# Placing the Gram products of a ConvNeXt-V2 block by the kind of slot, in portions of five

## The chip, the cores and the metric

The kernel runs on one core of one Trainium2 chip. The metric is the device time of one execution in microseconds. The engines are called TensorE (PE in the profile, its weight loads PEld), VectorE (DVE), ScalarE (ACT), GpSimd (POOL) and SyncE (SP, which issues DMAs). They run at the same time, each through its own instructions in program order, and wait for each other by semaphores.

## What is computed

One image of 512 x 512 pixels with C = 96 channels goes through a depthwise 3x3 convolution, a layer norm over channels, a matrix product to E = 384 channels, GELU, a global response normalization (GRN, which needs the sum of squares of each of the 384 channels over all pixels), and a product back to 96 channels, with the input added:

```python
out = sum over i, j of xp[:, i:i+H, j:j+W, :] * dw[i, j]      # depthwise 3x3
h = _layernorm(out)                                           # eps 1e-5
h = gelu(einsum('bhwc,ce->bhwe', h, w1))
gx = sqrt((h * h).sum(axis=(1, 2)) + 1e-6)
nx = gx / (gx.mean(axis=-1) + 1e-6)
h = grn_gamma * (h * nx) + grn_beta + h
return x + einsum('bhwe,ec->bhwc', h, w2)
```

## The kernel before

The image is cut into 128 blocks of four rows. Because GRN needs a sum over the whole image before the second product, the kernel has two parts. The first (to about 950 us of the span) does convolution, norm, first product, GELU and the sums of squares; the second makes the output, and makes most of the GELU output again. The change touches the first part.

The first part is a loop over slots s. In a slot the convolution works on block s, the first product and GELU on a block about 14 slots older, and the norm's steps on blocks between. The instructions of each engine stand in the order in which the code writes them (class `InOrder`), so the place of a call in the slot is its place in the engine's queue.

**PSUM.** The tile `PS` has eight banks of 512 f32 columns. Banks 0 to 3 take the first product's units, banks 4 to 6 the convolution's sums (`Y3`), bank 7 (`SG`, L398 to L400) two things: the norm's statistics `S` and the Gram sums `gram`.

**Units** (`unit`, L755). A block's first product is 12 banks, written as units 0 to 5 of one bank, unit 6 and unit 8 of two banks, and units 10 and 11 of one. After each, ScalarE makes one GELU pass over the one or two banks. Unit n lies in bank n mod 4, so it waits for the pass that emptied that bank.

**Taps** (`conv_taps`, L500 on; `conv` in the slot). The convolution is 72 small matmuls in three bursts of 24, called `conv(0)` ahead of unit 0, `conv(1)` behind unit 3 and `conv(2)` behind unit 6. In most slots `conv(1, u0)` waits for the GELU pass of unit 0 and `conv(2, u4)` for that of unit 4.

**Evacuation** (`evac`, L521). Behind the third burst the three banks of sums are copied to SBUF. There are two kinds of slot, told apart at L971: in a *shared* slot ScalarE copies two banks and VectorE the third; in the other kind, called a *three-bank slot* here, ScalarE copies all three in one pass. Which one a slot is depends on the block whose first product it makes: `cm_quads(b) == 2` makes it shared. From slot 20 on, counted by the last digit of that block's number, slots 0, 2, 3, 6 and 7 are three-bank slots and 1, 4, 5, 8 and 9 are shared. There are 54 three-bank slots from there to the end of the convolution; 33 follow a shared slot and 21 another three-bank slot.

**Sums of squares.** A block's GELU output comes in four quarters. For `cm_quads(b)` of them, channels lie on partitions and VectorE takes the sums (`squares`, `bn_stats`). For the rest pixels lie on partitions, and TensorE forms Gram products: a 128 x 128 matmul of a piece of the output with itself, added into `gram`, whose diagonal is wanted at the end. Each such quarter makes 12 Gram products, so a block makes 24, 12 or none. `owe_grams` (L815) puts them in a list when the block is done, and `gram_next(n)` (L808) writes the next n of the list into TensorE's queue, fewer if there are fewer. A block's output tile is one of five in a ring (`gpool`).

**Statistics.** In each slot 24 matmuls with `rowsel` add the norm's sums into `S` (`stage_stats`). Once in four slots VectorE copies `S` out and sets it to zero (`stage_moments`, the zeroing at L560). The first Gram product written after a zeroing waits for it, as both are in bank 7.

**The early slots.** Slots 5, 6, 8 and 9 make first products, slots 7 and 10 to 17 do not (the hole: the norm of the next blocks is not ready). A slot without units writes `gram_next(12)` first of all (L929), ahead of its taps. From slot 128 on there is no convolution, and up to 12 Gram products follow each unit (`mlp_tail`, L707).

Of the kernel before, what the change touches and what calls it, by code (L numbers as in the profile page):

```python
# [19 lines left out]
WHOLE = (0, 3, 7)  # L20
NTAIL = 14
GRB = 3
PORTION = 4


class InOrder:
# [31 lines left out]
def kernel(  # L58
# [40 lines left out]
    def is_whole(q):  # L99
        return q < TAIL0 and q % 10 in WHOLE or q == TAIL0  # L100
# [102 lines left out]
    with ExitStack() as p1:  # L203
# [428 lines left out]
        def stage_turn(k):  # L632
            NT = (BATCHES[k][1] * GR * NG + 31) // 32 * 32
            rt = rtpool.tile([128, NS], bf16, name="rt")
            dve.transpose(out=rt[:, :NT], in_=rns.pop(k)[:, :NT])
            rts[k] = rt
# [59 lines left out]
        def quarter(b, t):  # L696
            return gs[b][t] if isinstance(gs[b], list) else gs[b][:, t]
# [110 lines left out]
        def gram_next(n):  # L808
            for b, c0, j in grams[:n]:
                c = c0 % QC + j * 128  # L810
                v = quarter(b, c0 // QC).rearrange("p j w -> p (j w)")[:, c:c + 128]
                pe.matmul(gram[:, j, :], lhsT=v, rhs=v, start=False, stop=True, skip_group_check=True)
            del grams[:n]
# [37 lines left out]
        for k, (b0, n) in enumerate(BATCHES):  # L851
# [16 lines left out]
            for b in range(b0, b0 + n):  # L868
# [7 lines left out]
                put(m + is_whole(b), "combine", b)  # L876
                last_slot = m

        loaded = [4]
        busy(FILL[1])  # L880
        turn_x(0)
# [2 lines left out]
        for s in range(last_slot + 1):  # L884
            get = lambda kind: at.get((s, kind), [])
            early = s < AHEAD
            while loaded[0] < min(s + (6 if early else 5), NBLK):
                load_x(loaded[0])
                loaded[0] += 1
            if early:  # L890
                for b in get("read"):
                    stage_read(b)
            for k in get("rows"):
                stage_rows(k)
            for k in get("bcast"):
                stage_bcast(k)
            if not early:
                for b in get("read"):
                    stage_read(b)
            for b in get("write"):  # L900
                stage_write(b)
            if not HOLE <= s < HOLE + 4:
                store_next()
            if any(b >= TAIL0 for b in get("mlp")):
                store_next()
            for k in get("newton"):
                stage_newton(k, pool)
            for b in get("sqp"):
                stage_sq(b, False)
            for b in get("norm"):  # L910
                stage_norm(b)
            for k in get("rstd"):
                stage_rstd(k, pool)
            mlp = get("mlp")

            def spread_out(bank=0):
                for k in get("spread"):
                    stage_spread(k, bank)
                for b in get("norma"):
                    stage_norm(b, dve if b < 2 else pool)  # L920

            spare = not mlp and s % 2 == 1
            taps, evac = conv_taps(s, spare) if s < NBLK else ([], None)
            if mlp and mlp[0] >= TAIL0:
                assert not taps
                square_owed()
                mlp_tail(mlp[0], get)
            elif not mlp:
                gram_next(12)  # L929
                if s + 3 < NBLK and s != RAMP:  # L930
                    turn_x(s + 3)
                halves = [(b, h) for b in get("stats") if b >= RAMP for h in range(2)]
                for n, f in enumerate(taps):
                    f()
                    if n < 2:
                        for b, h in halves[:2 if len(halves) > 2 else 1]:
                            stage_stats(b, (h,))
                        del halves[:2 if len(halves) > 2 else 1]
                if not spare:
                    spread_out()  # L940
                if s == 3:
                    setup_mlp()
                if evac:
                    evac(s == RAMP)
                if s == RAMP:
                    turn_x(s + 3)
                for b in get("sqa"):
                    stage_sq(b, True)
                for b in get("stats"):
                    if b < RAMP:  # L950
                        stage_stats(b)
                for k in get("moments"):
                    stage_moments(k)
                if spare:
                    spread_out()
                for k in get("chain"):
                    stage_moments(k)
                    stage_chain(k)
                for k in get("turn"):
                    stage_turn(k)  # L960
                square_owed()
            else:
                b = mlp[0]
                unit, squares, squares_rest = mlp_units(b)
                lone = s - 1 not in mlp_slots

                def conv(n, behind=None):
                    if taps:
                        taps[n](lone, None if lone else behind)

                shared = evac is not None and (cm_quads(b) == 2 or s < HOLE)  # L971

                def turn():
                    if s + 3 < NBLK:
                        turn_x(s + 3)

                conv(0)
                u0 = unit(0, 1)
                unit(1, 1)
                if shared:  # L980
                    turn()
                    gram_next(PORTION)
                unit(2, 1)
                squares(0)
                gram_next(PORTION)
                unit(3, 1)
                conv(1, u0)
                spread_out(2)
                u4 = unit(4, 1)
                squares(1)  # L990
                gram_next(PORTION)
                unit(5, 1)
                if not shared:
                    turn()
                unit(6, 2)
                if not shared:
                    squares(2)
                    gram_next(PORTION)
                if s >= LATE:
                    for k in get("turn"):  # L1000
                        stage_turn(k)
                conv(2, u4)
                if evac:
                    evac(shared)
                if shared:
                    squares(2)
                else:
                    gram_next(PORTION)
                unit(8, 2)
                if shared:  # L1010
                    for b2 in get("stats"):
                        stage_stats(b2)
                unit(10, 1)
                if shared:
                    gram_next(PORTION)
                unit(11, 1)
                if not shared:
                    for b2 in get("stats"):
                        stage_stats(b2)
                for k in get("moments"):  # L1020
                    stage_moments(k)
                squares_rest(2)
                square_owed()
                if s < LATE:
                    for k in get("turn"):
                        stage_turn(k)
                if is_whole(b):
                    owed.append(lambda f=squares_rest: f(3))
                owe_grams(b, cm_quads(b) * QC, NQ * QC)
                if is_whole(b):  # L1030
                    stores.extend((b, h) for h in range(3))
            if s == 0:
                setup_ynt()
            if s == 4:
                setup_rest()
            if s == 6:
                for i in range(NI):
                    sp.dma_start(out=w1s[i:128:4], in_=w1p[i:C:NI])
            for b in get("combine"):
                combine(b)  # L1040
            if s == last_slot - 3:
                pc.close()
                late.gr = p2.enter_context(tc.tile_pool(name="gr", side="right", bufs=GRB))
                late.gh = p2.enter_context(tc.tile_pool(name="gh", side="right", bufs=1))
                late.xr = p2.enter_context(tc.tile_pool(name="xr", side="right", bufs=5))
                late.o = p2.enter_context(tc.tile_pool(name="o", side="right", bufs=6))
            if s == last_slot - 2:
                for n in range(XPRE):
                    load_xr(n, sp)
            if s == last_slot:  # L1050
                for n in range(PRE):
                    load_g(n, sp)
                for n in range(YPRE):
                    load_yn(n, sp)
# [109 lines left out]
```

## Time and profile before

| | us |
|---|---|
| median of 3 runs | 1436.2 (1435.39 to 1436.63) |
| the profiled execution | 1436.17 |
| its span in the profile | 1434.2 |
| TensorE busy | 1383.6 (96%) |
| ScalarE busy | 1380.3 (96%) |
| VectorE busy | 1306.3 (91%) |
| GpSimd busy | 887.8 (62%) |
| Gram products, 1632 of them, busy | 159.0 |
| three-bank evacuations from 100 to 865 us | 54, of 1.45 each |

Busy time is that in which an engine had at least one instruction under way. Matmuls overlap: one of 128 columns shows 0.22 us, but in a row the next one starts 0.056 us after it. For what work costs an engine, starts of neighbours are compared, not durations. The span is what the profile shows of an execution; the execution's own time is 2.0 us longer.

### The profile page before, as it was taken

Reading aid. Unit: us, or ns where it says so; the run is one execution under the profiler, and the core shown is the slowest. Engines: PE = TensorE matmul, PEld = TensorE weight load, DVE = VectorE, ACT = ScalarE, POOL = GpSimd, SP = SyncE. Lnnn points to the kernel's source line nnn. Section 1 sums busy time; section 2 is a strip of 40 time slices with the busy share of each in tenths; the row PEclk is TensorE's granted clock in tenths of the full one; section 3 lists DMA queues with packets and bytes.
Section 4 is the critical chain, followed back from the end, with each engine's and each line's share of the span. In section 5 each row is a group of like instructions: output and inputs, shape, how many; then the busy total and the mean of one; then the engine's idle time right before and its main releaser. Section 6 shows DMA issues by size and latency. Waiting matters only on the chain.

```text
span 1434.2 us, 54995 instructions
## 1 busy us (share of the span) xinstructions
PE 1383.6 (96%) x23332; PEld 829.0 (58%) x23332; DVE 1306.3 (91%) x2400; ACT 1380.3 (96%) x1693; POOL 887.8 (62%) x735
## 2 busy tenths in 40 slices
PE   8999999999999999999999997789999999999998
PEld 3445545555555555455545554467777777777776
DVE  8859999999999999999999998988888888888888
ACT  6889989999999999999999999999999999999997
POOL 2559999999998999999999997301111111111110
PEclk9999999999999999999999999999999999999999
DMA  6577899898888899999898987649999999999997
GB/s 194 169 219 222 248 285 274 259 276 271 258 261 251 268 266 272 290 262 268 258 278 270 266 249 221 187 166 411 415 384 412 404 414 398 414 390 392 397 397 279
DMA packets 167565, 423.65 MB, mean 295 GB/s; under 512 B 34166, under 2 KB 83766, under 8 KB 162710
## 3 DMA queue, kind: packets, MB, share of 16 engines
q1 hardware_dynamic: 151652, 314.59, 69.2%
q0 software_dynamic: 15104, 105.39, 18.5%
q8 instruction: 182, 2.98, 0.9%
q14 instruction: 65, 0.53, 0.1%
q10 hardware_dynamic: 562, 0.15, 0.0%
HBM read 262.16 MB, written 157.79 MB: 293 GB/s over the span
## 4 chain that ended last, share of the span: by engine, by line
PE 57%; ACT 19%; DVE 15%; DMA 4%; POOL 2%; issue 2%; SPq 1%; ACTq 0%; POOLq 0%; DVEq 0%
PE PS L36 57%; ACT g L36 14%; DVE bst L36 10%; ACT y_bf L36 4%; DVE xT L36 2%; DMA yn_dram<-yn 2%; DMA g_dram<-g 1%; POOL ysq L36 1%; POOL yn L36 1%; SPq L36 1%; DVE y_bf L36 1%; DVE o_sb L36 1%; DMA xin<-in_x_dram 0%; DVE mom L36 0%; ACT ysq L36 0%
## 5 line engine op out<-in xcount | busy, mean ns | idle before, releaser
L36 ACT ACTIVATE g<-PS 128x512 bf16<-128x512 f32 (+2 forms) x1160 | 704.1, 780 | 8.4 <-PE PS L36 8.1
L36 DVE BATCH_NORM_STATS2 bst<-g 128x6 f32<-128x512 bf16 x1020 | 622.5, 673 | 20.7 <-ACT g L36 20.4
L36 ACT ACTIVATE gr<-PS 128x1536 bf16<-128x1536 f32 x344 | 479.6, 1456 | 14.0 <-PE PS L36 7.8
L36 POOL TENSOR_TENSOR yn<-y_bf,rbc 128x1536 bf16<-128x1536 bf16 x126 | 391.4, 3108 | 61.6 <-ACT rbc L36 23.8
L36 PE MATMUL PS<-ynT,w1p 128*128 128x512 bf16 x1110 | 344.4, 383 | 19.4 <-ACT g L36 9.3
L36 PE MATMUL PS<-xT,Wq 64*32 64x511 bf16 (+1 forms) x9198 | 337.9, 387 | 7.4 <-ACT y_bf L36 0.8
L36 DVE TENSOR_TENSOR o_sb<-PS,B2c 128x384 bf16<-128x384 f32 x512 | 280.0, 555 | 58.4 <-PE PS L36 52.9
L36 POOL TENSOR_TENSOR ysq<-y_bf 128x1536 bf16<-128x1536 bf16 x114 | 313.3, 2748 | 26.0 <-ACT y_bf L36 20.0
L36 PEld LDWEIGHTS <-g 128*128 128x128 bf16 (+1 forms) x3603 | 218.3, 98 | 121.5 <-issue 39.6
L36 PE MATMUL PS<-ynT,w1s 128*128 128x512 bf16 x972 | 262.7, 379 | 0.0
L295 POOL DMA_DIRECT2D xr<-in_x_dram x116 | 62.2, 537 | 286.2 <-DVE o_sb L36 286.2
L36 PEld LDWEIGHTS <-gr 128*128 128x128 bf16 x4104 | 201.0, 98 | 53.8 <-issue 0.7
L36 PE MATMUL PS<-W2s,gr 128*128 128x96 bf16 x4032 | 209.8, 206 | 1.0 <-DVE o_sb L36 0.4
L36 ACT ACTIVATE y_bf<-PS 128x1536 bf16<-128x1536 f32 (+2 forms) x147 | 182.5, 1263 | 13.8 <-PE PS L36 13.2
L36 DVE STREAM_TRANSPOSE xT<-xin 128x576 f32<-128x576 f32 (+1 forms) x256 | 181.6, 749 | 11.0 <-PE PS L36 7.0
L36 PEld LDWEIGHTS <-w1p 128*128 128x128 bf16 x1110 | 95.5, 98 | 162.1 <-issue 114.3
L36 PEld LDWEIGHTS <-Wq 64*32 64x32 bf16 x9216 | 104.9, 90 | 127.4 <-ACT g L36 56.8
L36 PE MATMUL PS<-g 128*128 128x128 bf16 x1632 | 159.0, 220 | 6.4 <-DVE PS L36 5.8
L36 DVE TENSOR_TENSOR o_sb<-o_sb,xr 128x768 bf16<-128x768 bf16 x256 | 142.7, 557 | 8.9
L36 PE MATMUL PS<-w1p,ynT 128*128 128x384 bf16 (+1 forms) x924 | 141.6, 273 | 7.0 <-ACT y_bf L36 2.0
L36 PEld LDWEIGHTS <-ynT 128*128 128x128 bf16 x924 | 73.0, 97 | 59.1 <-issue 36.7
L36 PE MATMUL PS<-W2s,g 128*128 128x96 bf16 x1968 | 103.8, 206 | 0.2
(114 smaller groups left out, 660.3 us busy)
## 6 DMA issues: line engine op xcount, KB each, us to landing
g<-g_dram POOLq DMA_DIRECT2D x36, 1536.0 KB, 9.6
xin<-in_x_dram SPq DMA_DIRECT2D x126, 432.0 KB
g_dram<-g SPq DMA_DIRECT2D x105, 512.0 KB
yn_dram<-yn SPq DMA_DIRECT2D x512, 96.0 KB
ynT<-yn_dram SPq DMA_DIRECT2D x128, 384.0 KB
out_dram<-o_sb SPq DMA_DIRECT2D x127, 384.0 KB
xr<-in_x_dram POOLq DMA_DIRECT2D x124, 384.0 KB, 7.4
ynT<-yn_dram SPq DMA_DIRECT2D x243, 128.0 KB
```

The source lines that it names most:

```text
L36: r = f(*a, **k)
L295: pq.dma_start(out=xr[:], in_=x[0, r0:r0 + GR].rearrange("r w c -> (r w) c").rearrange("(p g) c -> p g c", g=PXP))
```

## The change

`PORTION`, the number of Gram products in a portion, goes from 4 to 5, and the portions move. A flag `was_shared` remembers whether the last slot with units was shared.

| place in the slot | before, shared | before, three-bank | after, shared | after, three-bank |
|---|---|---|---|---|
| behind unit 1 | 4 | | | |
| ahead of unit 3 | 4 | 4 | 5 behind a three-bank slot | 5 behind a three-bank slot |
| behind unit 4 | 4 | 4 | 5 | 5 |
| behind unit 6 | | 4 | | |
| behind the evacuation, ahead of unit 8 | | 4 | | 10 |
| behind unit 8 | | | | 5 |
| behind unit 10 | 4 | | | |

The list of owed products is never lost: what a slot does not write stays for the next. Over ten slots 144 products come in; before there is room for 160, after for 150. The list holds up to 32 between slots before, up to 56 after.

```diff
-PORTION = 4
+PORTION = 5
...
+        was_shared = False
...
                 unit(1, 1)
                 if shared:
                     turn()
-                    gram_next(PORTION)
                 unit(2, 1)
                 squares(0)
-                gram_next(PORTION)
+                if not was_shared:
+                    gram_next(PORTION)
                 unit(3, 1)
                 conv(1, u0)
...
                 unit(6, 2)
                 if not shared:
                     squares(2)
-                    gram_next(PORTION)
...
                 conv(2, u4)
                 if evac:
                     evac(shared)
                 if shared:
                     squares(2)
                 else:
+                    gram_next(2 * PORTION)
+                unit(8, 2)
+                if not shared:
                     gram_next(PORTION)
-                unit(8, 2)
                 if shared:
                     for b2 in get("stats"):
                         stage_stats(b2)
                 unit(10, 1)
-                if shared:
-                    gram_next(PORTION)
                 unit(11, 1)
...
+                was_shared = shared
```

No matmul is added or taken away, and the order of work on the other engines is the same.

## The prediction

> **What bounds the kernel now.** I read the stages first (busy time by stretch), then the groups of the steady stretch with shapes kept apart, then the order of time on TensorE and ScalarE over single slots, then the chain of waits in the early hole. The stretches:
>
> ```profile
> 150.00:400.00 250.00, 244.58 (x4462) 126.05 (x4446) 242.56 (x431) 245.52 (x391) 237.92 (x163) 0.99 0.90 267
> 400.00:650.00 250.00, 246.86 (x4525) 128.32 (x4517) 244.28 (x431) 248.46 (x395) 235.39 (x163) 1.00 0.91 268
> ```
>
> Columns: stretch, TensorE, its weight loads, VectorE, ScalarE, GpSimd busy, then clock and DMA. ScalarE is busy 98 to 99%, VectorE 97 to 98%. So a reordering on TensorE can gain at most what ScalarE idles, and loses as soon as TensorE falls behind ScalarE. The change moves Gram products alone: in the two builds' instruction order only TensorE's differs.
>
> The groups from 150 to 900 us (busy and mean ns, then idle time before and its releaser):
>
> ```profile
> L36 ACT ACTIVATE g<-PS 128x512 bf16<-128x512 f32 x818 | 420.3, 685 | 6.1 <-PE PS L36 5.7
> L36 PE MATMUL PS<-g 128*128 128x128 bf16 x1488 | 145.2, 220 | 6.1 <-DVE PS L36 5.8
> ```
>
> ScalarE's small idle time stands before one-bank passes, and TensorE's waits stand before Gram products, released by "DVE PS": the zeroing of the statistics (L560), which lie in the Gram products' PSUM bank. One such wait, on TensorE and then on VectorE:
>
> ```profile
> 320.80 0.82 PE L36 MATMUL PS<-ynT,w1p 128*128 128x512 bf16 x3
> 322.48 0.38 PE L36 MATMUL PS<-g 128*128 128x128 bf16 x4 [0.86 <-DVE PS L36]
> ...
> 322.27 0.17 DVE L36 MEMSET PS<- 128x128 f32 x1
> ```
>
> The first portion of this three-bank slot (behind a shared one) holds up the fourth unit and the second tap burst.
>
> Now a three-bank slot on TensorE, from its second tap burst to the next slot's:
>
> ```profile
> 510.19 0.88 PE L36 MATMUL PS<-xT,Wq 64*32 64x512 bf16 x24
> 511.01 0.39 PE L36 MATMUL PS<-ynT,w1p 128*128 128x512 bf16 x1
> 511.24 0.39 PE L36 MATMUL PS<-g 128*128 128x128 bf16 x4
> 511.46 0.81 PE L36 MATMUL PS<-ynT,w1p 128*128 128x512 bf16 x3
> 512.11 0.39 PE L36 MATMUL PS<-g 128*128 128x128 bf16 x4
> 512.42 0.87 PE L36 MATMUL PS<-xT,Wq 64*32 64x512 bf16 x24
> 513.23 0.40 PE L36 MATMUL PS<-g 128*128 128x128 bf16 x4
> 513.46 1.03 PE L36 MATMUL PS<-ynT,w1p 128*128 128x512 bf16 x4
> 514.33 0.45 PE L36 MATMUL PS<-rowsel,y_bf 128*128 128x4 bf16 x12
> ...
> 515.00 0.88 PE L36 MATMUL PS<-xT,Wq 64*32 64x512 bf16 x24
> 515.84 0.59 PE L36 MATMUL PS<-ynT,w1p 128*128 128x512 bf16 x2
> ```
>
> Starts are what counts, since ends overlap. Four Gram products take 0.22 us (0.056 each), a bank of units 0.216, a burst of taps 0.80 to 0.85, the 24 statistics 0.67, a switch from full tiles to taps 0.09. The second burst may not start before ScalarE has finished the slot's first unit (L987); here TensorE stood 0.13 us for that.
>
> **The change, part by part.** ScalarE's ends lie 0.49 us apart for one bank and 0.917 for two, in slot after slot; by that slope three banks are 1.344. Without a wait a three-bank slot is then 8 x 0.49 + 2 x 0.917 + 1.344 = 7.10 us and a shared one 8 x 0.49 + 3 x 0.917 = 6.67. From 103 to 865 us ScalarE's ends are 11.3 us later than that: 3.3 at the 54 three-bank evacuations, 0.8 at one late copy of VectorE (558 us), the rest at the zeroings, some 7.2 (the worst one, at 181.8 us, is 4.3).
>
> 1. *The evacuation.* In three-bank slots 8 products lay between the fifth unit and the third burst, now 5: the burst starts 3 x 0.056 = 0.17 us earlier. The evacuation started 0.13 to 0.16 us after the pass before allowed, so all 3.3 us come back. The burst's other condition (the fifth unit's pass) ends some 0.3 us before it in the trace and does not take over. Gain 3.3.
>
> 2. *The zeroing.* Behind a shared slot the portion ahead of the fourth unit is gone; the first product then stands behind the fifth unit, 0.75 (first pass) + 0.05 + 0.82 (burst) + 0.23 (unit) = 1.85 us after the slot's first pass starts. The zeroings end 0.3 to 1.2 us after that start, so six of the seven stalls go; the seventh ended at 2.96 and keeps about 1.1 us. Of 7.2 us 1.1 stay. Gain 6.1. In the other place (a shared slot behind a three-bank one) the zeroing ended about 0.7 us or more before the slot's first pass in all but one case, and nothing changes.
>
> 3. *The loop of a three-bank slot.* From its second burst to the next slot's it now carries 25 products: 5 behind the fifth unit, 10 behind the evacuation, 5 behind the two-bank unit, 5 ahead of the next fourth unit. From the rows: burst 0.82, unit 0.23, five products 0.28, three banks 0.65, switch 0.09, burst 0.81, ten products 0.57, four banks 0.86 with five products 0.28 inside, statistics 0.67, burst 0.84, three banks 0.65, five products 0.28, bank and switch 0.31: 7.34 us of unbroken TensorE work against ScalarE's 7.10. So TensorE becomes the bound here. Behind a shared slot (33 cases) TensorE had been waiting and starts level: the next slot's first unit is written at 5.27 + 0.84 = 6.11, its matmul ends 0.38 later, and a pass begins 0.04 after and takes 0.60: end at 7.13, due at 7.05, so 0.08 lost. The next second burst starts at 7.34 where 7.18 was allowed; the fifth unit ends 0.82 + 0.39 + 0.04 + 0.60 = 1.85 later, at 9.19, due at 7.13 + 4 x 0.49 = 9.09: 0.10 more. A three-bank slot behind another (21 cases) loses the whole 7.34 - 7.10 = 0.24. Cost 33 x 0.18 + 21 x 0.24 = 11.0. As a test of the sum, the trace's own unbroken stretch from that burst to the next slot's first unit, with 12 products in it, takes 5.64 to 5.68 us in four slots; the rows above give 5.27 + 0.84 - 8 x 0.056 = 5.66. With each loop 0.05 shorter the cost would be 33 x 0.08 + 21 x 0.19 = 6.6 (both halves of the 0.18 shrink), with 0.05 longer 33 x 0.28 + 21 x 0.29 = 15.3.
>
> 4. *The shared slots* shed their products (16 or fewer to 5). ScalarE was ahead of nothing there (no excess beyond 0.1 us in its ends); TensorE's loop falls to about 6.4 us against 6.67. It waits longer; gain 0.
>
> 5. *The hole* (slots 10 to 17, no units). Slots 8 and 9 now hand 14 products on; 12 of them open slot 10 and 2 slot 11. The chain of waits runs there through TensorE nearly without a break, from the zeroing on:
>
> ```profile
> 66.07 0.18 DVE PS L36
> 66.25 0.04 issue
> 66.29 1.24 PE PS L36 x29
> ```
>
> Before, slot 10's first burst (from 64.98) ran ahead of this zeroing and only the statistics waited. Now the products wait for it, and the burst is queued behind them on TensorE, and the statistics behind the burst: 12 x 0.056 + 0.09 + 1.0 (burst to statistics) = 1.75 us. The two of slot 11 add two switches, about 0.25. The zeroing itself comes from an unbroken row of VectorE work and is not moved. Cost 2.0. Cover: none, GpSimd was level with TensorE at the hole's end (an evacuation at 93.47 waited for it by 0.1) and so hides at most that much; the first pass behind the hole follows ScalarE's evacuation and square directly.
>
> The grant of the clock is a bound on this. In the trace it was halved for one window of 3.41 us after the 3.0 us wait at 181.8 and after a wait of 1.75 us at 864.7, not after waits of 1.2 us. The new wait at 65 to 66.3 is about 1.3 us, nearest the last: I take 0, with 1.7 (half a window) as the other end. [...]
>
> 6. *The end of the convolution* (slots 128, 129): 20 more products arrive. ScalarE idled 0.94, 0.47 and 0.21 us there while TensorE ran at half clock, so six more products at 0.107 us cost up to 0.7; but the fuller slot 127 shortens the 1.75 us wait that had halved the clock, which can give as much back. I take 0, from -0.7 to +0.7.
>
> Sum: -3.3 - 6.1 + 11.0 + 2.0 = +3.6. The profiled execution took 1436.17 us (span 1434.2), as good as the median of 1436.2: 1439.8.
>
> **The rivals.**
>
> *The loop has room after all* (the products fit behind the evacuation and TensorE is never late): 1436.2 - 3.3 - 6.1 + 2.0 = 1428.8, faster. For it: TensorE's 7.34 us is made of start distances, some of which may hide short waits. Against: the rows would have to shrink by 0.08 us and more, and the stretch that tests them varies by 0.04. It decides from a loop of 7.26 us down: there the cost is 33 x 0.02 + 21 x 0.16 = 4.0 and the sum -3.4. Chance 0.09.
>
> *Loss and gain cancel*: the loop is 0.05 shorter, cost 6.6 instead of 11.0 (1435.4), or the hole costs 1 us instead of 2 because GpSimd or a transfer sets its end after all (1438.8). For it: the sum is a small difference of larger terms. Chance 0.27.
>
> *The zeroing stays a wait.* With the stalls gone VectorE (idle 2 to 3%) loses the time in which it caught up; if it runs 1 us later, the products behind the fifth unit wait for it: six times about 0.5 us and the 0.7 us of a late copy twice, +4.5, 1444. For: its lag at this point already differs from 0.3 to 3.0. Against: three-bank slots become longer than they were, which gives VectorE its time back. Chance 0.08.
>
> *The clock halves in the hole*: 1439.8 + 1.7 = 1441.5. Chance 0.1.
>
> **How the numbers follow.** My forecast, the TensorE loop decides and the kernel gets slower as summed, has 0.46; with the last two rivals slower gets 0.62 (0.02 of the zeroing rival falls within the bound). Within 0.2% (2.9 us, about what a measurement of this kernel can tell from no change) 0.29, faster 0.09. The time is the likeliest case's, 1439.8; its own range, from the loop's 0.03 us either way and the ends of points 5 and 6, is 1439 to 1443.5 (what falls lower is the cancelling case). To leave out no more than 2 in 10, the range goes down to 1435.0, which takes in the cancelling case, and up to 1444.0.
>
> **What would show it.** Right: no TensorE wait of about 1 us on "DVE PS" ahead of Gram products in three-bank slots; three-bank evacuations that start on time; in runs of two three-bank slots a distance of 7.3 to 7.35 us between second bursts, with no wait of TensorE in between, and ScalarE's idle time before the fifth unit's pass; a first pass behind the hole near 98.4 instead of 96.4. Wrong: slots of 7.10 us there, or new waits on VectorE behind the fifth unit, or a hole of the old length.

## The result and the profile after

| | before | after |
|---|---|---|
| median of 20 runs each | 1434.94 us (1429.92 to 1438.37) | 1439.02 us (1435.54 to 1444.06) |
| profiled execution (its span) | 1436.17 us (1434.2) | 1439.77 us (1438.0) |

The ratio of the two, estimated from all the executions of both, is 1.0035, with a 95% interval of 1.0025 to 1.0044: the changed kernel is slower by 5.0 us (3.6 to 6.3). The two medians alone lie 4.1 us apart. The prediction was +3.6 us and 1439.8.

The stretches of the changed kernel's profile (stretch, then busy TensorE, weight loads, VectorE, ScalarE, GpSimd, then clock and DMA):

```profile
150.00:400.00 250.00, 246.36 (x4529) 125.02 (x4527) 245.00 (x435) 249.80 (x397) 236.53 (x163) 1.00 0.91 269
400.00:650.00 250.00, 246.49 (x4531) 125.16 (x4528) 245.31 (x433) 249.77 (x396) 235.71 (x163) 1.00 0.88 266
```

ScalarE now shows as busy without a gap (249.8 of 250), and yet the kernel is slower. The groups of the changed kernel from 150 to 900 us say the same:

```profile
L36 ACT ACTIVATE g<-PS 128x512 bf16<-128x512 f32 x826 | 431.6, 658 | 0.6
L36 PE MATMUL PS<-g 128*128 128x128 bf16 x1513 | 126.1, 219 | 0.0
```

The 6.1 us of idle time that stood before the one-bank passes and the 6.1 us before the Gram products, both of which the prediction started from, are gone. The one-bank passes are busy for 431.6 us instead of 420.3; some 4 us of that are 8 more passes inside the same window. The rest is lateness that doesn't show as idle time. In the records a pass starts ahead of the end of the one before: at the fifth unit of a three-bank slot behind another three-bank slot by 0.18 us before the change (mean of 21 slots), and its end comes 0.49 us after the end before. In the changed kernel that pass starts 0.01 us behind that end and its own end comes 0.60 us after it. A pass that is 0.1 us late thus loses overlap and adds to the busy time. What counts is when the passes end.

I therefore cut the time by ScalarE's records: the *hole stretch* runs from the start of slot 9's first GELU pass to the start of slot 18's, the *steady stretch* from there to the end of slot 127's last pass, the last slot with taps. In us, before and after: hole stretch 36.58 and 42.79, steady stretch 768.21 and 765.50, the rest behind it 569.6 and 568.6, with another 1.3 us ahead of slot 5. So the change gained 2.7 us in the steady stretch of these two executions and lost 6.2 in the hole. The experiments show that the two numbers vary, and that they depend on each other.

### The profile page after: what moved, and what is told of

It is laid out like the page before. It is cut to its first block, busy times and chain, and to the rows that moved or that the text cites. A ratio compares the mean times of both kernels' runs of the same rounds, so it can differ in the third digit from the quotient of the medians.

```text
span 1438.0 us, 54995 instructions
## 1 busy us (share of the span) xinstructions
PE 1383.1 (96%) x23332; PEld 819.6 (57%) x23332; DVE 1307.3 (91%) x2400; ACT 1383.3 (96%) x1693; POOL 887.7 (62%) x735
## 4 chain that ended last, share of the span: by engine, by line
PE 48%; ACT 27%; DVE 16%; DMA 4%; issue 3%; SPq 2%; POOL 1%; ACTq 0%; POOLq 0%
PE PS L36 48%; ACT g L36 20%; DVE bst L36 11%; ACT y_bf L36 6%; DVE xT L36 3%; DMA yn_dram<-yn 2%; SPq L36 2%; DMA rbc<-r_dram 1%; DVE y_bf L36 1%; POOL yn L36 1%; DVE o_sb L36 1%; ACT xT L36 1%; DMA xin<-in_x_dram 0%; ACT ysq L36 0%; DVE mom L36 0%
## 5 line engine op out<-in xcount | busy, mean ns | idle before, releaser
L36 ACT ACTIVATE g<-PS 128x512 bf16<-128x512 f32 (+2 forms) x1160 | 711.5, 757 | 3.8 <-PE PS L36 3.2
L36 PE MATMUL PS<-ynT,w1p 128*128 128x512 bf16 x1110 | 339.1, 382 | 24.9 <-ACT g L36 9.4
L36 PEld LDWEIGHTS <-g 128*128 128x128 bf16 (+1 forms) x3603 | 205.5, 98 | 89.7 <-issue 26.6
L36 DVE STREAM_TRANSPOSE xT<-xin 128x576 f32<-128x576 f32 (+1 forms) x256 | 181.8, 750 | 14.2 <-PE PS L36 14.0
L36 PE MATMUL PS<-g 128*128 128x128 bf16 x1632 | 135.9, 219 | 1.6 <-DVE PS L36 1.2
```

The costliest lines, as they stand in the source:

```text
L36: r = f(*a, **k)
```

## The experiments

"Late" below is the sum, over the steady stretch, of how much later than its ideal pace (7.10 us for a three-bank slot, 6.67 for a shared one) ScalarE ended its passes. Ratios are to the kernel before, run on the same chip beside each; the hole and steady columns come from each one's single profile.

| run | median, us | ratio (95% interval) | hole | steady | late |
|---|---|---|---|---|---|
| before | | | 36.58 | 768.21 | 11.3 |
| after | 1439.02 | 1.0035 (1.0025 to 1.0044) | 42.79 | 765.50 | 8.5 |
| after_again | 1437.57 | 1.0041 (1.0029 to 1.0053) | 40.26 | 764.90 | 7.9 |
| e1_early_as_before | 1433.48 | 1.0003 (0.9991 to 1.0015) | 37.75 | 767.71 | 10.8 |
| e2_ahead_moved | 1433.27 | 0.9995 (0.9982 to 1.0008) | 42.81 | 759.21 | 2.3 |
| e3_evac_only | 1431.47 | 0.9989 (0.9976 to 1.0002) | 40.33 | 761.21 | 4.3 |
| e4_evac_and_zero | 1428.55 | 0.9964 (0.9949 to 0.9978) | 36.57 | 760.37 | 3.4 |
| e5_both | 1426.48 | 0.9970 (0.9959 to 0.9982) | 36.68 | 761.25 | 4.3 |
| e6_hole_only | 1435.37 | 1.0033 (1.0017 to 1.0049) | 40.74 | 763.06 | 6.1 |
| e6_hole_only_again | 1434.10 | 1.0005 (0.9992 to 1.0018) | 41.74 | 763.14 | 6.2 |
| e8_hole_behind_taps | 1434.55 | 1.0000 (0.9986 to 1.0013) | 40.41 | 763.45 | 6.5 |
| e9_ahead_three | 1427.31 | 0.9958 (0.9943 to 0.9974) | 36.62 | 761.99 | 5.0 |

**Early slots as before.** The changed kernel, with the old portions of four in the slots ahead of the hole, so that no products are left for it:

```diff
+                    if s < HOLE:
+                        gram_next(4)
                 unit(2, 1)
                 squares(0)
+                if s < HOLE:
+                    gram_next(4)
...
-                gram_next(PORTION)
+                gram_next(4 if s < HOLE else PORTION)
                 unit(5, 1)
...
                 unit(10, 1)
+                if s < HOLE:
+                    gram_next(4)
```

> The changed kernel, with slots 5 to 9 placing their Gram products as the kernel before did, so that none is handed on to the hole. Theory: the 12 products opening slot 10 and the 2 opening slot 11 cost 2.1 us on TensorE (1.75 for the first, because the first tap burst and the statistics are queued behind them and behind the zeroing; 0.35 for the second, as the profile of the changed kernel shows); the rest of the hole's 6.2 us in that profile is chance (TensorE waits of 1.46 and 1.13 us without a releaser, and a window of half clock). So about 2 us faster than the changed kernel, still some 2 us slower than the kernel before, first pass behind the hole 36.5 to 38 us after slot 9's (before 36.6, changed 42.8). Rival (the hole is the whole loss): 6 us faster than the changed kernel, equal to or faster than the kernel before.

Measured: 1.0003, against 1.0035 and 1.0041 for the changed kernel. The hole stretch falls from 42.8 to 37.8 us. What is left of the change comes out level with the kernel before (its interval is -1.3 to +2.2 us), nearer to the rival than to the theory; that the hole is not the whole loss is shown by the next experiments. The late sum of its profile, 10.8, holds two stalls of 2.1 us together that the two profiles of the changed kernel lack. Both are waits of TensorE for the zeroing, 0.45 us behind a fifth unit at 182.0 us and 0.70 ahead of a fourth unit at 237.7.

**The portion ahead of the next fourth unit moved.** The changed kernel, with that portion written behind unit 10 of shared slots:

```diff
-                if not was_shared:
-                    gram_next(PORTION)
                 unit(3, 1)
...
                 unit(10, 1)
+                if shared and s >= HOLE:
+                    gram_next(PORTION)
```

> The changed kernel with one portion moved: the 5 products ahead of the next fourth unit go behind unit 10 of the shared slots. The loop of a three-bank slot then holds 20 products: 7.34 - 0.28 = 7.06 us against ScalarE's 7.10. Theory: the 8.7 us by which ScalarE's ends are late behind three-bank slots in the profile of the changed kernel (0.04 to 0.12 at the next first pass, 0.09 to 0.14 at the next fifth) fall to nearly nothing, so 7 to 8.7 us faster than the changed kernel and 3 to 5 us faster than the kernel before; the shared slots, 0.2 us short of their limit, take the 5 at no cost. Rival (the loss lies in the ten behind the evacuation, or in the hole alone): same as the changed kernel within 1 us. Rival (a shared slot has no room): the loss moves there, 24 to 56 times 0.1 us.

Measured: 0.9995 (0.9982 to 1.0008), so moving five products out of the three-bank slot's loop takes back some 6 us; the late sum falls from 8.5 to 2.3. The 3 to 5 us against the kernel before did not come. Its hole keeps the products and is as long as that of the changed kernel (42.81), and in this one execution the rest behind the steady stretch took 571.9 us, where the other profiles have 568.6 to 569.8; nothing in the edit explains that.

**The evacuation alone.** The kernel before, with the portion behind unit 6 written behind the evacuation:

```diff
                     squares(2)
-                    gram_next(PORTION)
...
-                    gram_next(PORTION)
+                    gram_next(2 * PORTION)
                 unit(8, 2)
```

> The kernel before with one part of the change: in three-bank slots the portion of 4 behind unit 6 goes behind the evacuation (8 there, still 4 each). Theory: the third burst starts 0.22 us earlier, the 54 evacuations start on time, their 3.3 us of late ends go: 3 us faster than the kernel before. TensorE's loop keeps 16 products, 6.9 us, below ScalarE's 7.10. The stalls at the zeroing stay. Rival (ScalarE makes up for late evacuations anyway): no difference.

Measured: 0.9989 (0.9976 to 1.0002), which wall time alone doesn't tell from no change. In its profile no evacuation starts late any more: the 3.3 us of lateness there are gone. The zeroing still stops TensorE, as TensorE's and VectorE's order of time in this kernel shows, in the same slot as in the prediction:

```profile
320.22 0.82 PE L36 MATMUL PS<-ynT,w1p 128*128 128x512 bf16 x3
322.00 0.38 PE L36 MATMUL PS<-g 128*128 128x128 bf16 x4 [0.96 <-DVE PS L36]
...
321.78 0.17 DVE L36 MEMSET PS<- 128x128 f32 x1
```

**The evacuation and the zeroing.** The same, and in three-bank slots behind a shared one the portion ahead of unit 3 goes behind the evacuation too (the flag `was_shared` is that of the change):

```diff
+                late_one = was_shared and not shared
+                if not late_one:
+                    gram_next(PORTION)
                 unit(3, 1)
...
-                    gram_next(2 * PORTION)
+                    gram_next((3 if late_one else 2) * PORTION)
```

> The run with the evacuation part alone, and besides, in three-bank slots behind a shared one, the portion ahead of the fourth unit goes behind the evacuation too (12 there), so that the first product after a zeroing stands behind the fifth unit. Theory: the stalls on the zeroing (7.2 us of late ends in the profile of the kernel before, 4.3 of them in one place) go: 3 to 6 us faster than the evacuation part alone, 6 to 9 faster than the kernel before. Rival (the wait only moves, behind the fifth unit): as the evacuation part alone.

Measured: 0.9964, faster by 5.2 us (3.2 to 7.3), somewhat less than the 6 to 9 expected. The same slot in its order of time:

```profile
318.92 1.15 PE L36 MATMUL PS<-ynT,w1p 128*128 128x512 bf16 x4
320.19 0.86 PE L36 MATMUL PS<-xT,Wq 64*32 64x512 bf16 x24
320.98 0.39 PE L36 MATMUL PS<-ynT,w1p 128*128 128x512 bf16 x1
321.21 0.39 PE L36 MATMUL PS<-g 128*128 128x128 bf16 x4
...
320.44 0.17 DVE L36 MEMSET PS<- 128x128 f32 x1
```

Four units in a row, the second burst, and then products whose zeroing ended 0.6 us earlier: the wait has no place left. Of ScalarE's lateness 1.05 us (in the slot from 180.4 us) stays, at a zeroing behind a fifth unit, the place where the prediction let 1.1 us stay. Another 1.2 us is a wait for a transfer just behind the hole, in slot 19.

**Both mends of the changed kernel.** Early slots as before, and the portion moved:

```diff
-                if not was_shared:
-                    gram_next(PORTION)
+                if s < HOLE:
+                    gram_next(4)
                 unit(3, 1)
...
                 unit(10, 1)
+                if shared:
+                    gram_next(4 if s < HOLE else PORTION)
```

(and the other lines of the first experiment)

> The changed kernel with both repairs: the portion ahead of the next fourth unit behind unit 10 of the shared slots, and the early slots as before. Theory (loop and hole are the two costs, and add): steady stretch 759 us as in the run with the portion moved (changed kernel 765.5), hole 36.6 to 38 us, plus what chance adds; 6 to 9 us faster than the kernel before, 10 faster than the changed kernel. Rival (the hole's length is chance and not its products): as the run with the portion moved, same as the kernel before within 1 us.

Measured: 0.9970, faster than the kernel before by 4.3 us (2.6 to 5.9), short of the 6 to 9 expected. The hole is as short as expected; the steady stretch is 761.25 us and not 759, with two waits of 0.46 us for the zeroing behind fifth units (at 179.3 and 207.6 us), which make ScalarE 1.7 us late. With either mend alone the ratio was about 1.000: from these ratios, taken on different chips and each uncertain by 1.3 to 1.9 us, the loss in the hole is worth 3.6 to 5.4 us and that in the loop 4.7 to 6.6, and together they outweigh the change's gains.

**The hole alone.** The kernel before, with only five products behind unit 4 in the slots ahead of the hole, so that 14 are left for it as in the change:

```diff
-                    gram_next(PORTION)
+                    if s >= HOLE:
+                        gram_next(PORTION)
                 unit(2, 1)
                 squares(0)
-                gram_next(PORTION)
+                if s >= HOLE:
+                    gram_next(PORTION)
...
-                gram_next(PORTION)
+                gram_next(5 if s < HOLE else PORTION)
...
-                if shared:
+                if shared and s >= HOLE:
                     gram_next(PORTION)
```

> The kernel before, with the early slots alone as the change has them (5 products in each of slots 8 and 9, 12 and 2 handed on to slots 10 and 11). Theory: 2.1 us slower than the kernel before, with the hole at 38.7 us plus chance. Rival (the longer wait in slot 10 brings more with it: in both profiles with these products the hole took 42.8 us, with TensorE waits of 1 to 1.5 us that no engine ended and a window of half clock): 5 to 6 us slower, hole near 42.8 again.

> The kernel before with the early slots of the change, again, beside the other on the same chip. Theory: 2.3 us from the products and the wait, and waits without a releaser of 1.7 to 3.9 us as in the other four profiles with this order: 3 to 5 us slower than the kernel before. Rival (those waits were chance): below 0.5 us in this profile.

> The changed kernel once more, beside the runs with its two repairs on the same chip. Theory: 5 us slower than the kernel before, as first measured; steady stretch 765 to 767 us, and the hole between 38.7 and 43, as the waits without a releaser fall. Rival (the hole is always 42.8): 42.8 again.

Measured: 1.0033 and, on another chip, 1.0005; the changed kernel beside the first of them 1.0041. A loss from the hole is shown by the first of them; its size in wall time is not settled better than by these two values, 4.7 and 0.7 us. The second is a miss: 3 to 5 us were expected. The hole stretch was 40.7 and 41.7 us.

From slot 18 on these two and the next run have the order of the kernel before, yet all three profiles have a steady stretch of 763.1 to 763.5 us, where before has 768.2. So in their profiles the steady stretch gives back nearly all that the hole takes: both together are 803.8 to 804.9 us, and 804.8 before. What goes with the difference is a wait of VectorE for GpSimd, most of it at about 111 us, behind the hole. In the profile of before it reads (us in all, times, longest, from 100 to 870 us):

```profile
DVE rt L36 <- POOL rstd L36: 2.7, 2, 2.4
```

After a hole of 36.6 to 37.8 us (five profiles: before, e1, e4, e5, e9) VectorE waits there 2.1 to 3.1 us in all for GpSimd, and the zeroing that slot 30's products wait for ends 2.3 to 3.0 us after the start of that slot's first pass. After a hole of 40.3 us or more (the other seven) the wait is not in the list, and that zeroing ends 0.8 to 1.4 us after it. The run with the evacuation alone has a long hole without products and is among the seven, so this goes with the length of the hole. No experiment set that length by itself, so that a longer hole lets GpSimd catch up is argued and not shown.

**The hole's products behind the taps.** The hole alone again, but slots 10 and 11 write their products behind the third burst instead of first of all:

```diff
-                gram_next(12)
+                if s not in (HOLE, HOLE + 1):
+                    gram_next(12)
...
+                if s in (HOLE, HOLE + 1):
+                    gram_next(12)
                 if not spare:
```

> As the run with the hole's part alone, but slots 10 and 11 write their 12 and 2 products behind the third tap burst instead of ahead of the first. Theory (half of the cost is that the first burst can no longer run while TensorE waits for the zeroing): from the zeroing's release to the first unit behind the hole, less waits without a releaser, 28.9 to 29.3 us (28.0 without the products, 30.3 to 30.8 with them in front), and 1 us slower than the kernel before. Rival (the products' own time is all that counts): 30.3 again. If the waits without a releaser, 1.7 to 3.9 us in the four profiles with the products in front and mostly 0.2 to 1.4 in the five without, come from the long wait in slot 10, they are small here; if they come by chance or from the products, they stay.

Measured: 1.0000 (0.9986 to 1.0013), not to be told from the hole alone beside it (1.0005) in wall time. In the traces it can be told, within the hole. TensorE's order of time with the products first (the hole alone):

```profile
65.07 0.83 PE L36 MATMUL PS<-g 128*128 128x128 bf16 x12 [1.21 <-DVE PS L36]
65.83 0.87 PE L36 MATMUL PS<-xT,Wq 64*32 64x512 bf16 x24
66.82 0.45 PE L36 MATMUL PS<-rowsel,y_bf 128*128 128x4 bf16 x12
...
81.56 0.85 PE L36 MATMUL PS<-xT,Wq 64*32 64x512 bf16 x19
83.55 0.41 PE L36 MATMUL PS<-xT,Wq 64*32 64x511 bf16 x5 [1.14 <-issue]
```

and behind the taps:

```profile
64.69 0.87 PE L36 MATMUL PS<-xT,Wq 64*32 64x512 bf16 x24
65.97 0.44 PE L36 MATMUL PS<-rowsel,y_bf 128*128 128x4 bf16 x12 [0.41 <-DVE PS L36]
...
68.52 0.84 PE L36 MATMUL PS<-g 128*128 128x128 bf16 x12
...
81.28 0.85 PE L36 MATMUL PS<-xT,Wq 64*32 64x512 bf16 x19
83.28 0.41 PE L36 MATMUL PS<-xT,Wq 64*32 64x511 bf16 x5 [1.15 <-issue]
```

With the products first, the taps and the statistics start 1.75 us (66.82 - 65.07) behind the zeroing's release; behind the taps only the statistics wait, as before the change. From that release to the first unit behind the hole, with the time lost to waits without a releaser ("issue") and to half clock taken off, the six profiles without products in the hole need 28.0 to 28.3 us, the five with the products first 30.3 to 30.8, this one 29.5, between what theory and rival gave. So the products cost 2.0 to 2.8 us, of which about 1.1 is the queue behind the zeroing and the rest the products and the switches between tile shapes (0.76 us for twelve products and the switch to taps, 65.07 to 65.83).

**Three instead of five ahead of the next fourth unit.** The first experiment, with three products there and two behind unit 10 of shared slots:

```diff
                 if not was_shared:
-                    gram_next(PORTION)
+                    gram_next(3)
...
-                if s < HOLE:
-                    gram_next(4)
+                if shared:
+                    gram_next(4 if s < HOLE else 2)
```

> The changed kernel with early slots as before, and 3 instead of 5 products ahead of the next fourth unit, the 2 behind unit 10 of shared slots. The loop of a three-bank slot has 23 products: 7.23 us. Theory: the late fifth units (0.035 to 0.137 us each at 25 products, none at 20) lose 0.11 each, and the late first passes behind a run of two fall too: ScalarE's ends 3 to 4.5 us late in the steady stretch without stalls, between 2.3 (20 products) and 7.9 to 8.7 (25), and 3 to 6 us faster than the kernel before. Rival (the loss is per product and has no threshold): halfway, 5.5 to 6.

Measured: 0.9958 (0.9943 to 0.9974), faster by 6.0 us (3.7 to 8.2). Two products fewer in the loop suffice: the late sum is 5.0, and 3.7 without two stalls in the slots from 176 and 205 us, which are waits for the zeroing behind fifth units again (0.34 and 0.46 us). This kernel, the evacuation with the zeroing, and the two mends together beat both kernels; which of the three is fastest their intervals don't tell.

## Why the prediction came out right

The direction and the two causes of the loss, the loop and the hole, were as forecast, and the experiments that take away one cause, the other or both bear them out. That the time came out so well is in good part luck. For the steady stretch the terms -3.3, -6.1 and +11.0 gave +1.6 us; against the profile that the prediction started from, the two profiles of the changed kernel have -2.7 and -3.3. For the hole the sum had +2.0; they have +6.2 and +3.7. The two errors offset each other.

**The evacuation (-3.3): right.** ScalarE's order of time in the changed kernel, start and duration:

```profile
475.70 1.02 ACT L36 ACTIVATE g<-PS 128x1024 bf16<-128x1024 f32 x1
476.61 1.46 ACT L36 ACTIVATE y_bf<-PS 128x1536 bf16<-128x1536 f32 x1
477.94 1.05 ACT L36 ACTIVATE g<-PS 128x1024 bf16<-128x1024 f32 x1
```

The evacuation starts 0.11 us ahead of the end of the pass before (476.72), and the next pass 0.13 us ahead of the evacuation's end: ScalarE takes them one behind the other, and nothing is missing. The sum of lateness there is nothing after, 3.3 us in the profile of before and 2.8 in the hole alone.

**The zeroing (-6.1): right in kind, but not independent of the hole.** TensorE's waits for "DVE PS" from 100 to 870 us (in all, times, longest) were, in the kernel before,

```profile
PE PS L36 <- DVE PS L36: 5.8, 7, 2.6
```

and in the hole alone, which has the same order there,

```profile
PE PS L36 <- DVE PS L36: 2.9, 4, 0.9
```

The changed kernel's list has no such line, so against the profile of before all 7.2 us of lateness are gone, and not 6.1. But the 2.6 us wait at 181.8 (the prediction, where it speaks of the clock, calls it 3.0), with 4.3 us of ScalarE's lateness, belongs to the short hole: the three profiles with the order of before and a long hole have 3.4 to 3.8 us of lateness at zeroings. Moving the products takes back that much; the rest of the 7.2 went with the longer hole. The run with the early slots as before, a short hole and the order of the change behind it, keeps 2.1 us. The prediction treated the hole and the zeroing as separate terms, and put what a longer hole saves behind it at nothing.

**TensorE's loop (+11.0): right in kind, too large.** TensorE in a three-bank slot of the changed kernel behind another one, from second burst to second burst:

```profile
473.44 0.92 PE L36 MATMUL PS<-xT,Wq 64*32 64x512 bf16 x24
474.29 0.39 PE L36 MATMUL PS<-ynT,w1p 128*128 128x512 bf16 x1
474.51 0.44 PE L36 MATMUL PS<-g 128*128 128x128 bf16 x5
474.79 0.81 PE L36 MATMUL PS<-ynT,w1p 128*128 128x512 bf16 x3
475.54 0.87 PE L36 MATMUL PS<-xT,Wq 64*32 64x512 bf16 x24
476.34 0.73 PE L36 MATMUL PS<-g 128*128 128x128 bf16 x10
...
479.55 0.82 PE L36 MATMUL PS<-ynT,w1p 128*128 128x512 bf16 x3
480.21 0.44 PE L36 MATMUL PS<-g 128*128 128x128 bf16 x5
480.49 0.38 PE L36 MATMUL PS<-ynT,w1p 128*128 128x512 bf16 x1
480.80 0.87 PE L36 MATMUL PS<-xT,Wq 64*32 64x512 bf16 x24
```

No bracket, so no wait, and 480.80 - 473.44 = 7.36 us, where 7.34 was worked out. The idle time of ScalarE ahead of the fifth unit's pass that the prediction gave as a sign does not show (0.6 us before all one-bank passes together); the lateness shows in the ends. From the end of one slot's first pass to that of the next, ScalarE's records give these medians:

| this slot, the next one | ideal | before | after | e9_ahead_three |
|---|---|---|---|---|
| three-bank behind shared, any | 7.10 | 7.15 | 7.15 | 7.14 |
| three-bank behind three-bank, any | 7.10 | 7.15 | 7.32 | 7.20 |
| shared behind three-bank | 6.67 | 6.67 | 6.76 | 6.67 |
| shared behind shared | 6.67 | 6.67 | 6.67 | 6.67 |

The first kind loses 0.05 and, at the fifth unit of the slot behind it, 0.09, where the sum had 0.08 and 0.10; the second loses 0.22 (mean 0.24), where it had 0.24. In all 8.5 and 7.9 us in two profiles instead of 11.0. Moving the portion ahead of the next fourth unit took this back (e2_ahead_moved), and 25, 23 and 20 products in the loop leave about 8, 3.7 and 2.3 us of lateness without the stalls, which shows the cause. Against the three profiles with the order of before and a hole as long, the steady stretch is 765.5 and 764.9 us against 763.1 to 763.5: 1.5 to 2.4 us longer.

**The shared slots (0): right**, by the last row of the table.

**The hole (+2.0): right in kind, too small.** TensorE in the changed kernel:

```profile
67.63 0.83 PE L36 MATMUL PS<-g 128*128 128x128 bf16 x12 [1.22 <-DVE PS L36]
68.39 0.87 PE L36 MATMUL PS<-xT,Wq 64*32 64x512 bf16 x24
69.39 0.45 PE L36 MATMUL PS<-rowsel,y_bf 128*128 128x4 bf16 x12
...
71.94 0.29 PE L36 MATMUL PS<-g 128*128 128x128 bf16 x2
...
81.72 0.44 PE L36 MATMUL PS<-rowsel,y_bf 128*128 128x4 bf16 x12 [1.46 <-issue]
```

The first burst waits behind the products and the statistics start 1.76 us after the release, as worked out (1.75), and the two products of slot 11 stand where they were said to. The net cost of the products was 2.0 to 2.8 us. The end is set by TensorE still, as ScalarE's last evacuation in the hole shows (the bracket is the idle time before it):

```profile
101.02 1.51 ACT L36 ACTIVATE y_bf<-PS 128x1024 bf16<-128x1024 f32 x2 [0.53 <-PE PS L36]
102.56 1.48 ACT L36 ACTIVATE ysq<-y_bf 128x1536 bf16<-128x1536 bf16 x1
103.95 2.52 ACT L36 ACTIVATE g<-PS 128x512 bf16<-128x512 f32 x5
```

The first pass behind the hole starts at 103.95, not near 98.4. Of the 7.5 us against the 96.41 of before, 1.3 were there ahead of slot 5 already, about 2.3 are the products and what they hold up, and about 3.9 are two waits without a releaser (1.46 and 1.13 us) and a stretch of half clock (1.3), of which the last section tells. In six profiles with products in the hole such waits add up to 1.4 to 2.6 us (mean 1.9), in six without to 0 to 2.6 (mean 0.7), and stretches of half clock fall into three of the six and one of the six. Whether the products cause the difference was not settled. These waits were in no term of the sum, and neither was what the longer hole gives back behind it. How the measured 5.0 us divide is therefore known only roughly; that both the loop and the hole cost time is shown by the ratios of the experiments.

**The rivals.** *The loop has room* fell: 7.36 us, without a wait. *Loss and gain cancel* had the right reason, a small difference of larger terms, but the loop was not shorter (it cost about 8 us instead of 11 all the same) and the hole not cheaper. *The zeroing stays a wait* did not happen in the two profiles of the changed kernel, which both have a long hole. With the short one it did: its repaired versions e1, e5 and e9 have two such waits each, of 0.3 to 0.7 us, which cost 1.3 to 2.1 us in lateness, less than the 4.5 of the rival. *The clock halves in the hole*: not behind the wait that the prediction named, at 66.4 to 67.6 us, as the stretch behind it shows, but in one of the two profiles 21 us later. Three stretches of the changed kernel (the columns as above; the clock is the last but two):

```profile
67.60:71.00 3.40, 3.13 (x82) 1.78 (x82) 3.40 (x6) 0.45 (x1) 2.99 (x7) 1.00 0.00 0
...
85.30:88.70 3.40, 2.17 (x64) 1.12 (x68) 0.50 (x1) 2.13 (x3) 2.82 (x9) 1.00 0.28 65
88.70:92.10 3.40, 3.29 (x76) 1.43 (x68) 1.56 (x3) 2.32 (x2) 3.23 (x4) 0.50 0.76 234
```

**The clock (0) and the end of the convolution (0).** The stretch of half clock at 88.7 cost about 1.3 us (the two bursts take 2.65 us to the start of the statistics behind them instead of 1.67, the next burst 1.29 instead of 0.99). The second profile of the changed kernel has none in the hole, while e2_ahead_moved has two of them in a row and the second run of the hole alone has one: 0 was the value of three of six profiles. The rest of the execution took 568.6 and 569.0 us against 569.6: no loss at the end.

## What to carry to other kernels

When two engines are nearly level, count the work between two dependences of a loop (here from one second burst to the next) and not the work per slot: ten slots had room for all the products, but one kind of slot was 0.24 us over, and moving two products of its 25 to the other kind was enough (from a ratio of 1.0003 to 0.9958). Before two terms are added, ask whether they depend on each other: the largest stall on record, 4.3 us of lateness, came with a short hole and went with a long one, so part of the time lost in the hole was won back behind it. And the Gram products, which share a PSUM bank with VectorE's zeroing, waited for it (7 times from 100 to 870 us in the profile of before, 5.8 us in all) and so brought VectorE's queue into TensorE's, for everything written behind them; put such work last where the write may be late, not first (0.8 to 1.3 us within the hole, seen in the traces and not in wall time).

## What the runs showed of the hardware that was not expected

TensorE waits in the hole for which the profile names no releaser. In the changed kernel 1.46 us ahead of 81.72 are put down to "issue" (shown above), and at 87.50 it stops within one burst, after 19 of 24 taps:

```profile
85.52 0.85 PE L36 MATMUL PS<-xT,Wq 64*32 64x512 bf16 x19
87.50 0.41 PE L36 MATMUL PS<-xT,Wq 64*32 64x511 bf16 x5 [1.13 <-issue]
88.01 0.45 PE L36 MATMUL PS<-rowsel,ysq 128*128 128x4 bf16 x12
88.39 2.54 PE L36 MATMUL PS<-xT,Wq 64*32 64x512 bf16 x48
```

The same tap of the same burst in the hole alone and in the version behind the taps has 1.14 and 1.15 us (both shown above). Since the long wait for the zeroing is absent in the latter, it is not their cause. Nor do they need the products: the evacuation alone, without any in the hole, has two of 0.33 and 2.24 us and a stretch of half clock behind the second (95.36 to 98.77 us), which is why its hole stretch is 40.3 us. Most stand in two fixed places: nine of the twelve profiles wait 0.2 to 1.7 us at the tap of 87.50, and five 0.3 to 2.2 us at one later tap (94.57 in the second profile of the changed kernel). What causes them stays open.

The clock halves after less idle time than expected. The 48 taps at 88.39 take 2.54 us, and mostly 1.55 elsewhere, with a clock of 0.50 from 88.70 to 92.10 (above). The wait ahead of them was 1.13 us, shorter than the 1.75 us that the profile of before showed, while a wait of 1.14 us at 82.4 in the hole alone (clock 1.00 from 83.6 to 87.0) and the 1.22 us wait at 66.4 (1.00 from 67.6 to 71.0) cost no clock. In the second run of the hole alone 0.85 us, ahead of 81.73, was followed by half clock from 82.66 to 86.07, which is 3.41 us. Ahead of the end of its span, the profile of before has three halved stretches, which start at 29.03, 182.63 and 865.30 us and last 6.83, 3.41 and 3.41 us; their starts are 153.60 and 682.67 us apart, 45 and 200 times 3.413. The busy share ahead does not explain why similar waits differ: TensorE was busy for 2.17 of the 3.40 us ahead of the halving (the stretch from 85.30 above), and in the same trace, from 78.47 to 81.88, for only 1.95 us, with the 1.46 us wait inside, after which the clock stayed whole (1.00 from 81.88 to 85.30). What decides stays open.
